# A DFT-plus-MLP kernel: the first-stage output stored as [chunk, residue, feature] instead of [feature, chunk, residue]

## The chip, the cores and the metric

The kernel runs on one core of one Trainium2 chip. The time is the device time of one execution in microseconds (us); lower is better. A profile of one execution stands beside the times.

## The reference, cut to what matters

For each of 8 batches of 3072 rows and 256 features the reference takes a Fourier transform along the rows, then one along the features, and keeps the real part. The 24576 resulting rows go through a small network: the elementwise maximum of three matrix products, then an output product.

```
X = fft(x, axis=1); X = fft(X, axis=2); a = X.real      # x: 8 x 3072 x 256
h = max(a @ w1, a @ w2, a @ w3)                         # 256 -> 768
out = h @ w_out                                         # 768 -> 256
```

## The kernel before, in words

The row transform of length 3072 is split as 24 x 128. The feature axis is split into four chunks `g` of 64 features `dl` each. For every batch the function `fnet` does three steps and then the network runs on its result.

First stage (lines 267 to 272). For each of the 64 features, one matmul with 128 columns of `x0` as its weights and the small block matrix `m24blk` as moving data gives 96 numbers per partition: 4 chunks `g` times 24 residues `r`. The weights are taken from `x0` with a step of 64 elements, 128 bytes. Five features (once four) share a PSUM tile `ps1`, and one ScalarE (ACT) copy moves the 480 numbers to the SBUF tile `ub` as bf16. There are 13 such evictions in a batch, in the order of `DLS`, and the PSUM pool `ps_f` has two buffers, so matmul group n+2 waits for eviction n. In `ub` the 96 numbers of a feature lie together.

Folds (lines 279 to 297). VectorE (DVE) adds and subtracts mirrored features: `fold` combines features `lo..hi` of chunk `g` with features `64-lo..64-hi`, backwards, of chunk `3-g`. The sums go to `zE`, the differences to `zO`. There are three rounds (25 features, two times 10, two times 9), each for two chunks, sums before differences; five small operations (lines 289 to 297) finish feature 0.

Second stage (lines 305 to 335). For each residue `r` the 128 folded features of that residue are the weights of a matmul, `er[:, :, r]` or `orr[:, :, r]`, with cosine or sine tables as moving data (128 columns, 64 for two residues). In the layout of before, neighbouring weights of one residue are 24 elements apart in `zE` (48 bytes) and 26 apart in `zO` (52 bytes). There are 50 such matmuls a batch in six PSUM tiles `ps2` of the same pool `ps_f`, each evicted by ACT to `tE` or `tO` (line 329), and three more with one column (lines 332 to 334). GpSimd then makes reversed copies (lines 339 and 340).

The network (`unit_plus`, `unit_minus`, `unit_out`, `l2_half`, `l2_block`) works in three blocks a batch: TensorE fills `pse`, ACT takes a relu to `stmp` (line 363), DVE takes the maximum into `hp` or `hm` (line 364), and the output product accumulates in `po` (lines 367, 369, 372), is copied by DVE to `ot` (line 392) and stored from the SP queue. A scheduler interleaves output-product matmuls of the batch before with the first and second stage of the next batch. Each engine then works through its own list in that order.

At the start DVE and ACT build the tables. The order in which `zE` and `zO` hold the 128 features must match the order in the tables `md`; that order comes from `dvec` (line 130).

Of the kernel before, what the change touches and what calls it, by code (L numbers as in the profile page):

```python
# [34 lines left out]
def kernel(  # L35
# [16 lines left out]
    nc = tc.nc  # L52
# [44 lines left out]
    def load_x0(b, between):  # L97
        x0 = x0_pool.tile([96, 128 * 64], BF16, name="x0", tag="x0")
        xr = x[b].rearrange("(a bb) (g dl) -> g a bb dl", bb=128, g=4)
        x0v = x0.rearrange("p (bb dl) -> p bb dl", dl=64)  # L100
        for ch in range(4):
            if ch in between:
                between[ch]()
            for g in range(4):
                nc.gpsimd.dma_start(  # L105
                    out=x0v[g * 24:(g + 1) * 24, ch * 32:(ch + 1) * 32, :],
                    in_=xr[g, :, ch * 32:(ch + 1) * 32, :])
        return x0
# [15 lines left out]
    dvec = gen.tile([128, 128], FP32, tag="dvec")  # L124

    def between():

        nc.gpsimd.iota(kidx, [[1, 13], [24, 128]], base=0, channel_multiplier=0,
                       allow_small_or_imprecise_dtypes=True)
        nc.gpsimd.iota(dvec, [[1, 64], [64, 2]], base=0, channel_multiplier=0,  # L130
                       allow_small_or_imprecise_dtypes=True)

    with tc.manual_schedule(engines={mybir.EngineType.Pool}):
# [3 lines left out]
        for jh in range(2):  # L137
            for wsrc, wdst in ((moe_w1, w1_bf), (moe_w2, w2_bf), (moe_w3, w3_bf)):
                nc.gpsimd.dma_start(
                    out=wdst.rearrange("p (fc j) -> p fc j", fc=2)[:, :, jh * 384:(jh + 1) * 384],  # L140
                    in_=wsrc.rearrange("(fc p) j -> p fc j", fc=2)[:, :, jh * 384:(jh + 1) * 384])
        nc.gpsimd.dma_start(out=wout_bf.rearrange("p (jc c) -> p jc c", jc=NJC),
                            in_=moe_w_out.rearrange("(jc p) c -> p jc c", jc=NJC))
# [5 lines left out]
    for thr in (48, 24):  # L149
# [3 lines left out]
                                   in1=pidx[0:96], op0=ALU.mult, op1=ALU.add)  # L153
# [60 lines left out]
    zO_tiles = [consts.tile([128, 128 * 26], BF16, name=f"zO{i}", tag=f"zO{i}")  # L214
                for i in range(1)]
    for zO in zO_tiles:
        nc.vector.memset(zO.rearrange("p (c r) -> p c r", r=26)[:, :, 24:26], 0.0)
        nc.vector.memset(zO[:, 0:26], 0.0)

    def prep_first():  # L220

# [42 lines left out]
    def fnet(b, x0):  # L264
        x0r = x0.rearrange("p (bb dl) -> p bb dl", dl=64)
        ub = u_pool.tile([128, 64 * 96], BF16, name="ub", tag="ub")
        for (d0, d1) in DLS:
            ps1 = ps_f.tile([128, 512], FP32, name="ps1", tag="ps")
            for i in range(d1 - d0):
                nc.tensor.matmul(ps1[:, i * 96:(i + 1) * 96], x0r[:, :, d0 + i], m24blk,  # L270
                                 start=True, stop=True)
            nc.scalar.copy(out=ub[:, d0 * 96:d1 * 96], in_=ps1[:, 0:(d1 - d0) * 96])  # L272

        u = ub.rearrange("p (dl g r) -> p dl g r", g=4, r=24)
        zE = z_pool.tile([128, 128 * 24], BF16, name="zE", tag="zE")
        zO = zO_tiles[b % len(zO_tiles)]
        e = zE.rearrange("p (dl g r) -> p dl g r", g=2, r=24)
        o = zO.rearrange("p (dl g r) -> p dl g r", g=2, r=26)
        def fold(dst, op, lo, hi, g):
            nc.vector.tensor_tensor(out=dst[:, lo:hi, g, 0:24], in0=u[:, lo:hi, g, :],  # L280
                                    in1=u[:, 64 - lo:64 - hi:-1, 3 - g, :], op=op)

        for ranges in (((20, 45),), ((10, 20), (45, 55)), ((1, 10), (55, 64))):
            for (dst, op) in ((e, ALU.add), (o, ALU.subtract)):
                for (lo, hi) in ranges:
                    for g in range(2):
                        fold(dst, op, lo, hi, g)
                if ranges[0][0] == 1:
                    nc.vector.tensor_tensor(out=dst[:, 0, 1, 0:24], in0=u[:, 0, 1, :],
                                            in1=u[:, 0, 3, :], op=op)  # L290
                    if dst is e:
                        nc.vector.tensor_copy(e[:, 0, 0, :], u[:, 0, 0, :])

        nc.vector.tensor_scalar(out=o[:, 0, 0, 1:12], in0=u[:, 0, 2, 13:24], scalar1=-1.0,
                                scalar2=None, op0=ALU.mult)
        nc.vector.tensor_copy(o[:, 0, 0, 13:24], u[:, 0, 2, 1:12])
        nc.vector.tensor_copy(o[:, 0, 0, 24:26], u[:, 0, 2, 0:13:12])

        er = zE.rearrange("p (c r) -> p c r", r=24)
        orr = zO.rearrange("p (c r) -> p c r", r=26)  # L300

        def iO(r):
            return 24 if r == 0 else 25 if r == 12 else 12 + r

        tE = t_pool.tile([128, NHALF], BF16, name="tE", tag="tE")
        tO = t_pool.tile([128, NHALF], BF16, name="tO", tag="tO")
        for (tile_i, dst) in ((0, tE), (1, tO)):
            for g in range(3):
                parts = [(r, r * 128, 128) for r in range(4 * g + 1, min(4 * g + 5, 12))]
                if g == 2:  # L310
                    parts += [(0, 0, 64), (12, 12 * 128, 64)]
                ps2 = ps_f.tile([128, 512], FP32, name="ps2", tag="ps")
                c0 = 0
                for (r, k0, w) in parts:
                    outsl = ps2[:, c0:c0 + w]
                    if tile_i == 0:
                        two = 1 <= r <= 11
                        nc.tensor.matmul(outsl, er[:, :, r], cos_t[:, k0:k0 + w],  # L318
                                         start=True, stop=not two)
                        if two:  # L320
                            nc.tensor.matmul(outsl, er[:, :, 12 + r], sin_t[:, k0:k0 + w],  # L321
                                             start=False, stop=True)
                    else:
                        nc.tensor.matmul(outsl, orr[:, :, r], nsin_t[:, k0:k0 + w],  # L324
                                         start=True, stop=False)
                        nc.tensor.matmul(outsl, orr[:, :, iO(r)], cos_t[:, k0:k0 + w],  # L326
                                         start=False, stop=True)
                    c0 += w
                nc.scalar.copy(out=dst[:, g * 512:(g + 1) * 512], in_=ps2)  # L329

        ps3 = ps_f.tile([128, 512], FP32, name="ps3", tag="ps")
        nc.tensor.matmul(ps3[:, 0:1], er[:, :, 0], cos_t[:, 64:65], start=True, stop=True)
        nc.tensor.matmul(ps3[:, 1:2], orr[:, :, 0], nsin_t[:, 64:65], start=True, stop=False)
        nc.tensor.matmul(ps3[:, 1:2], orr[:, :, 24], cos_t[:, 64:65], start=False, stop=True)
        nc.scalar.copy(out=t_mid[:, :, b], in_=ps3[:, 0:2])

        tEr = t_pool.tile([128, NHALF], BF16, name="tEr", tag="tEr")
        tOr = t_pool.tile([128, NHALF], BF16, name="tOr", tag="tOr")
        nc.gpsimd.tensor_copy(tEr, tE[:, ::-1])  # L339
        nc.gpsimd.tensor_copy(tOr, tO[:, ::-1])  # L340
        return (tE, tO), (tEr, tOr)
# [83 lines left out]

    for b in range(B):
        tt = fnet(b, x0_tiles.pop(b))
        if b == 0:
            prep_first()
# [60 lines left out]
```

## Time and profile before

| | us |
|---|---|
| median of three runs | 500.57 |
| lowest, highest | 499.67, 501.51 |
| span of the profiled execution | 497.1 |
| PE busy, share of the span | 453.5, 91% |
| DVE busy | 320.4, 64% |
| ACT busy | 260.9, 52% |
| POOL busy | 140.6, 28% |

The span runs from the first to the last instruction of the profiled execution. No separate total was recorded for that execution; the median of the runs stands 3.5 us above its span, for what lies around it. In the rows of the profile, PE is a TensorE matmul and PEld a weight load; a group row gives line, engine, operation, output and inputs with their shapes, the count, then the busy time in us and the mean of one in ns, then the idle time of the engine just before and what ended it. In a timeline row the first two numbers are the start and the duration in us; where several instructions are merged (x2), the duration is from the first start to the last end.

### The profile page before, as it was taken

To read this page: it belongs to the slowest core of one execution; us is meant where nothing else is said; L and a number is where in the kernel's file an instruction comes from. 1 tells how busy PE (TensorE), PEld (TensorE's weight loads), DVE (VectorE), ACT (ScalarE), POOL (GpSimd) and SP (SyncE) were. 2 spreads that over 40 slices of the span, in tenths; PEclk is the share of its full clock that TensorE was granted. 3 is DMA by queue.
4 is the path that set the end of the run, shared out by engine and by line. 5 is a ranking of instruction groups with operands and counts; after the bars stand their busy time and mean duration, and the time that the engine had idled before them with its cause. 6 is when DMAs were issued, how large, how long until landed. Compare 5 with 4: busy or idle time off the path is not lost.

```text
span 497.1 us, 9195 instructions
## 1 busy us (share of the span) xinstructions
PE 453.5 (91%) x3408; PEld 315.6 (63%) x3408; DVE 320.4 (64%) x662; ACT 260.9 (52%) x472; POOL 140.6 (28%) x160
## 2 busy tenths in 40 slices
PE   0056999999999999999999999999999999999995
PEld 0055447785568657785669666875669566866664
DVE  8834674657676576657666567657675666667663
ACT  1355652575436653575446644665457644765440
POOL 9979800029000750029000840048000100020000
PEclk9999899999999999999999999999999999999998
DMA  8999992219921692219911793119911022102122
GB/s 48 75 164 99 98 32 86 84 44 108 105 86 66 59 133 99 73 44 109 126 65 65 74 123 102 65 46 120 134 64 65 22 65 84 65 22 65 65 84 86
DMA packets 163436, 40.05 MB, mean 81 GB/s; under 512 B 136512, under 2 KB 163392, under 8 KB 163392
## 3 DMA queue, kind: packets, MB, share of 16 engines
q0 software_dynamic: 135536, 14.30, 70.6%
q1 hardware_dynamic: 27856, 25.18, 16.1%
q8 instruction: 26, 0.43, 0.4%
q14 instruction: 18, 0.15, 0.1%
HBM read 28.31 MB, written 25.17 MB: 108 GB/s over the span
## 4 chain that ended last, share of the span: by engine, by line
PE 78%; DVE 3%; ACT 2%; POOL 2%; DMA 1%; issue 1%; DVEq 0%; ACTq 0%
PE po L372 23%; PE pse L349 12%; PE pse L357 11%; PE pse L350 11%; PE ps L270 8%; PE po L367 4%; PE po L369 4%; POOL x L105 2%; PE ps L318 2%; DMA x<-in_x_dram 1%; PE ps L324 1%; PE ps L326 1%; ACT stmp L363 1%; PE ps L321 1%; DVE zE L280 1%
## 5 line engine op out<-in xcount | busy, mean ns | idle before, releaser
L363 ACT ACTIVATE stmp<-pse 128x512 bf16<-128x512 f32 (+1 forms) x294 | 167.7, 588 | 164.3 <-PE pse L350 128.6
L364 DVE TENSOR_TENSOR hp<-pse,stmp 128x512 bf16<-128x512 f32 x144 | 99.1, 690 | 99.1 <-PE pse L357 39.8
L105 POOL DMA_DIRECT2D x<-in_x_dram x128 | 109.5, 863 | 8.1 <-DMA x<-in_x_dram 3.6
L349 PE MATMUL pse<-tE,gE 128*128 128x512 bf16 x288 | 108.8, 379 | 1.7 <-DVE hm L364 0.7
L350 PE MATMUL pse<-tO,gO 128*128 128x512 bf16 x288 | 109.1, 380 | 0.0
L364 DVE TENSOR_TENSOR hm<-pse,stmp 128x512 bf16<-128x512 f32 x144 | 99.0, 687 | 11.8 <-ACT stmp L363 9.3
L357 PE MATMUL pse<-tO,gD 128*128 128x512 bf16 x288 | 94.8, 380 | 1.1 <-ACT stmp L363 0.6
L339 POOL COPY tEr<-tE 128x1536 bf16<-128x1536 bf16 x8 | 11.8, 1471 | 289.1 <-ACT tE L329 289.1
L372 PE MATMUL po<-wout_bf,hp 128*128 128x256 bf16 x576 | 92.6, 272 | 0.0
L372 PE MATMUL po<-wout_bf,hm 128*128 128x256 bf16 x576 | 89.1, 272 | 0.1
L270 PE MATMUL ps<-m24blk,x 96*128 96x96 bf16 x512 | 57.4, 250 | 28.8 <-DMA w_bf<-in_moe_w_dram 27.5
L270 PEld LDWEIGHTS <-x 96*128 96x128 bf16 x512 | 55.9, 199 | 33.1 <-DMA w_bf<-in_moe_w_dram 27.4
L392 DVE COPY ot<-po 128x512 f32<-128x512 f32 x96 | 65.5, 684 | 14.5 <-PE po L372 13.8
L372 PEld LDWEIGHTS <-hm 128*128 128x128 bf16 x576 | 56.1, 99 | 17.3 <-DVE hm L364 0.4
L372 PEld LDWEIGHTS <-hp 128*128 128x128 bf16 x576 | 56.2, 100 | 14.2
L272 ACT CAST ub<-ps 128x480 bf16<-128x480 f32 (+1 forms) x104 | 55.4, 554 | 15.6 <-PE ps L270 13.3
L357 PEld LDWEIGHTS <-gD 128*128 128x128 bf16 x288 | 28.1, 98 | 29.8 <-issue 1.5
L350 PEld LDWEIGHTS <-gO 128*128 128x128 bf16 x300 | 29.4, 98 | 27.1 <-issue 12.2
L349 PEld LDWEIGHTS <-gE 128*128 128x128 bf16 x300 | 29.5, 99 | 21.1 <-issue 2.6
L280 DVE TENSOR_TENSOR zE<-ub 128x240 bf16<-128x240 bf16 (+2 forms) x80 | 20.2, 311 | 33.9 <-ACT ub L272 33.9
L367 PE MATMUL po<-gw,tE 128*128 128x256 bf16 x96 | 26.2, 272 | 0.0
L369 PE MATMUL po<-gwr,tOr 128*128 128x256 bf16 x96 | 26.2, 272 | 0.0
(99 smaller groups left out, 359.5 us busy)
## 6 DMA issues: line engine op xcount, KB each, us to landing
out_dram<-ot SPq DMA_DIRECT2D x176, 128.0 KB, 1.7
x<-in_x_dram POOLq DMA_DIRECT2D x128, 96.0 KB, 6.7
out_dram<-ot SPq DMA_DIRECT2D x24, 64.0 KB, 6.7
w_bf<-in_moe_w_dram POOLq DMA_DIRECT2D x6, 192.0 KB, 6.2
out_dram<-ot SPq DMA_DIRECT2D x8, 63.0 KB
wout_bf<-in_moe_w_out_dram POOLq DMA_DIRECT2D x1, 384.0 KB, 8.6
out_dram<-ot SPq DMA_DIRECT2D x1, 8.0 KB
```

The source lines that it names most:

```text
L105: nc.gpsimd.dma_start(out=x0v[g * 24:(g + 1) * 24, ch * 32:(ch + 1) * 32, :], in_=xr[g, :, ch * 32:(ch + 1) * 32, :])
L270: nc.tensor.matmul(ps1[:, i * 96:(i + 1) * 96], x0r[:, :, d0 + i], m24blk, start=True, stop=True)
L272: nc.scalar.copy(out=ub[:, d0 * 96:d1 * 96], in_=ps1[:, 0:(d1 - d0) * 96])
L349: nc.tensor.matmul(pse[:, 0:n], gE[i][:, js], te, start=True, stop=False)
L350: nc.tensor.matmul(pse[:, 0:n], gO[i][:, js], to, start=False, stop=True)
L357: nc.tensor.matmul(pse, gD[i][:, js], to, start=False, stop=True, skip_group_check=True)
L363: nc.scalar.activation(out=stmp[:, 0:n], in_=pses[0][:, 0:n], func=AX.Relu)
L364: nc.vector.tensor_tensor(out=dst, in0=src3, in1=stmp[:, 0:n], op=ALU.max)
L367: nc.tensor.matmul(po, te, gw[:, 0:256], start=True, stop=False)
L369: nc.tensor.matmul(po, to, wo, start=False, stop=False)
L372: nc.tensor.matmul(po, hcols(jc), wout_bf[:, jc * 256:(jc + 1) * 256], start=False, stop=(jc == NJC - 1))
L392: nc.vector.tensor_copy(out=ot, in_=po)
```

## The change

`ub` becomes [chunk, residue, feature], so that the 64 features of one chunk and residue lie together. ACT still reads a PSUM tile from end to end but now writes each number 64 elements (128 bytes) from the one before. `zE` and `zO` become [residue, feature]: the 128 weights of one residue lie together. The fold's innermost loop runs over features instead of residues: its rows have 25, 10 or 9 elements instead of 24, and its second input runs backwards with step -1 inside a row. The number of instructions of every kind is unchanged. The memsets of the constant parts of `zO` and the feature order in `dvec` follow the layout.

```diff
-        nc.gpsimd.iota(dvec, [[1, 64], [64, 2]], base=0, channel_multiplier=0,
+        nc.gpsimd.iota(dvec, [[1, 128]], base=0, channel_multiplier=0,
...
-        nc.vector.memset(zO.rearrange("p (c r) -> p c r", r=26)[:, :, 24:26], 0.0)
-        nc.vector.memset(zO[:, 0:26], 0.0)
+        zOr = zO.rearrange("p (r c) -> p r c", c=128)
+        nc.vector.memset(zOr[:, 24:26, :], 0.0)
+        nc.vector.memset(zOr[:, :, 0:1], 0.0)
...
+        ubd = ub.rearrange("p (gr dl) -> p dl gr", dl=64)
...
-            nc.scalar.copy(out=ub[:, d0 * 96:d1 * 96], in_=ps1[:, 0:(d1 - d0) * 96])
-
-        u = ub.rearrange("p (dl g r) -> p dl g r", g=4, r=24)
+            nc.scalar.copy(out=ubd[:, d0:d1, :],
+                           in_=ps1[:, 0:(d1 - d0) * 96].rearrange("p (dl gr) -> p dl gr", gr=96))
+
+        u = ub.rearrange("p (g r dl) -> p dl g r", g=4, r=24)
...
-        e = zE.rearrange("p (dl g r) -> p dl g r", g=2, r=24)
-        o = zO.rearrange("p (dl g r) -> p dl g r", g=2, r=26)
+        e = zE.rearrange("p (r g dl) -> p dl g r", g=2, dl=64)
+        o = zO.rearrange("p (r g dl) -> p dl g r", g=2, dl=64)
         def fold(dst, op, lo, hi, g):
-            nc.vector.tensor_tensor(out=dst[:, lo:hi, g, 0:24], in0=u[:, lo:hi, g, :],
-                                    in1=u[:, 64 - lo:64 - hi:-1, 3 - g, :], op=op)
+            nc.vector.tensor_tensor(
+                out=dst[:, lo:hi, g, 0:24].rearrange("p dl r -> p r dl"),
+                in0=u[:, lo:hi, g, :].rearrange("p dl r -> p r dl"),
+                in1=u[:, 64 - lo:64 - hi:-1, 3 - g, :].rearrange("p dl r -> p r dl"), op=op)
...
-        er = zE.rearrange("p (c r) -> p c r", r=24)
-        orr = zO.rearrange("p (c r) -> p c r", r=26)
+        er = zE.rearrange("p (r c) -> p c r", c=128)
+        orr = zO.rearrange("p (r c) -> p c r", c=128)
```

## The prediction

> **What bounds the kernel now.** I read first the chain that ended last, then who waited for whom, then the groups with their shapes kept apart, and last the timeline of the first and second stage of two batches. The chain:
>
> ```profile
> PE 78%; DVE 3%; ACT 2%; POOL 2%; DMA 1%; issue 1%; DVEq 0%; ACTq 0%
> ```
>
> TensorE is the bound: nearly all of the end is set by its own work, and in the middle of the kernel it hardly idles. So a matmul that starts sooner is worth its whole time, and any new wait of PE costs its whole length. Two waits show where PE meets the changed code:
>
> ```profile
> PE ps L270 <- ACT ub L272: 1.3, 6, 0.3
> PEld L318 <- DVE zE L292: 4.7, 8, 1.8
> ```
>
> Columns are total us, times, longest. The first is PE waiting for an eviction before it can refill `ps_f`; the second is the second stage waiting for the last sums, in every batch. Both are short now and both have no cover left.
>
> The timeline (start, duration) of batch 0, where nothing is interleaved, then of the third batch, then two loads of neighbouring weights from the end:
>
> ```profile
> 28.15 1.02 ACT L272 CAST ub<-ps 128x480 bf16<-128x480 f32 x2 [5.09 <-PE ps L270]
> 28.76 1.06 PE L270 MATMUL ps<-m24blk,x 96*128 96x96 bf16 x10 [0.21 <-ACT ub L272]
> 29.40 1.02 ACT L272 CAST ub<-ps 128x480 bf16<-128x480 f32 x2 [0.22 <-PE ps L270]
> ```
>
> ```profile
> 152.04 1.02 ACT L272 CAST ub<-ps 128x480 bf16<-128x480 f32 x2
> 153.19 0.56 PEld L270 LDWEIGHTS <-x 96*128 96x128 bf16 x5
> 153.62 0.19 PEld L372 LDWEIGHTS <-hp 128*128 128x128 bf16 x2
> 159.65 0.56 ACT L272 CAST ub<-ps 128x480 bf16<-128x480 f32 x1 [0.29 <-PE ps L270]
> 161.27 0.15 PEld L318 LDWEIGHTS <-zE 128*128 128x128 bf16 x1 [0.41 <-DVE zE L292]
> 162.38 0.11 PEld L372 LDWEIGHTS <-hp 128*128 128x128 bf16 x1
> 480.39 0.17 PE L349 MATMUL pse<-t_mid,gE 128*128 128x8 bf16 x1
> 480.42 0.17 PE L350 MATMUL pse<-t_mid,gO 128*128 128x8 bf16 x1
> ```
>
> The loop of the first stage can be read off batch 0. The first eviction of a pair ends at 28.71; PE starts the next ten matmuls 0.05 us later; ACT gets the first of them at 29.40, which is 0.64 us on. A pair of evictions therefore takes 0.56 + 0.05 + 0.64 = 1.25 us, and 13 evictions 6.5 x 1.25 = 8.1 us. The third batch takes the same: 152.04 to 159.65 + 0.56 is 8.2. ACT is busy for 1.02 of each 1.25 us, so it is close to being the bound of this stage.
>
> The groups that I price from:
>
> ```profile
> L272 ACT CAST ub<-ps 128x480 bf16<-128x480 f32 x96 | 52.0, 560 | 15.6 <-PE ps L270 13.3
> L272 ACT CAST ub<-ps 128x384 bf16<-128x384 f32 x8 | 3.9, 481 | 0.0
> L280 DVE TENSOR_TENSOR zE<-ub 128x600 bf16<-128x600 bf16 x16 | 6.8, 468 | 24.5 <-ACT ub L272 24.5
> L280 DVE TENSOR_TENSOR zE<-ub 128x216 bf16<-128x216 bf16 x32 | 6.5, 266 | 6.6 <-ACT ub L272 6.6
> L364 DVE TENSOR_TENSOR hm<-pse,stmp 128x512 bf16<-128x512 f32 x144 | 99.0, 687 | 11.8 <-ACT stmp L363 9.3
> L217 DVE MEMSET zO<- 128x128 uint32 x1 | 0.2, 165 | 0.1
> L218 DVE MEMSET zO<- 128x13 uint32 x1 | 0.1, 69 | 0.0
> L122 DVE MEMSET neg_pi<- 128x1 f32 x1 | 0.1, 59 | 0.8 <-PEq L474 0.8
> ```
>
> **The change part by part.** The built program has the same instructions in the same order on every engine, with the same waits; only addresses and steps move. No DMA and no queue is touched.
>
> *Second stage, removed cost.* Its weight loads of 48- and 52-byte steps stand (162.38 - 161.27) / 16 = 69 ns apart. Neighbouring weights, at 480.39 and 480.42, stand about 32 ns apart with a matmul of 8 columns; a matmul of 256 columns runs every 109 ns (the product matmuls of line 372), so one of 128 should take about 55. Per batch 44 matmuls fall from 69 to 55 ns (0.62 us), six of 64 columns and three of one column from 69 to some 32 (0.33): at most 0.9 us. But each group of eight hands its tile to a 586 ns eviction of line 329 in the same two buffers, and a pair of groups then takes eviction + 0.05 + 8 matmuls + drain, in which only the eight matmuls shrink, 0.11 us a pair, three pairs and the first group: 0.4 us. I take 0.5. Batch 0 gains nothing: its 128-column matmuls stand 107 ns apart whatever the load. 7 x 0.5 = 3.5 us off, between 2.8 and 6.3.
>
> *First stage, added cost.* The two L272 rows give ACT 0.82 ns an element and 165 ns fixed, and two evictions in a row overlap by 0.10 us (2 x 0.56 - 1.02). The new writes step 128 bytes. No ACT row of the trace does that, so let the 0.82 grow by a factor k: an eviction takes E = 165 + 395k ns, and a pair takes E + 0.69 us, or 2 (E - 0.10) once E passes 0.89. There is no slack: the loop is a cycle through the eviction.
>
> The near rows disagree on k. For none: the memset of 128 words at 52-byte steps takes 165 ns, 0.83 ns for each word over the 59 of a single word, and that of 13 adjacent words takes 69, also 0.83. For a high price: TensorE's loads. The `x0` weights have just this 128-byte step in bf16 and stand (153.62 - 153.19) / 5 = 86 ns apart against 32 for neighbours, k = 2.7; the `zE` weights at 48 bytes give 69 / 32 = 2.1. These are reads of another engine, but of the same memory, type and step, and there are hundreds of them where the memsets are one each; I take the middle, 2.4, and keep 1 and 2.7 as ends.
>
> With k = 2.4, E = 1.11 us (0.92 for the short one). ACT becomes the bound: 12 x 1.01 + 0.82 + 0.10 = 13.0 us against 8.1, 4.9 more a batch, 39.5 us over eight. At k = 2 it is 3.0 a batch (24 us), at 2.7 it is 6.0 (48 us). All of it reaches PE: behind the last L270 group PE has only some 1.7 us of product matmuls, which the last two evictions and the folds outlast, and PE's list is fixed, so nothing else moves into the hole.
>
> The Trainium skill, Vector Engine (DVE) Microarchitecture Reference, section 5.2, has measured a VectorE stream whose destination alone steps 24 words: 2.50 to 2.51 ns a column against 1.054 for adjacent ones. It speaks against this change where the memset row speaks for it: by the row the evictions stay at 0.56 us and the sum is about -1.5 us; by that page, carried over to ScalarE as an estimate, it is about +37. No run here shows yet which.
>
> *Folds.* 600 elements take 468 ns and 216 take 266, so 0.53 ns an element; an operation on three bf16 operands with a backward step inside its rows is not in the trace (the reversed write of line 364 costs nothing, 687 ns, but it reads PSUM and runs at a lower rate). If the new rows lose the doubled rate, 216 elements take about 115 ns more. Only the last four sums stand between the last eviction and the second stage, with L289 and L292 behind: 0.46 + some 0.05 us, 4.1 us over eight batches. The earlier folds and the differences have DVE idle time before them (24.5 us ahead of the first). Ends 0 and 4.1; I take 2.
>
> *The rest.* The memsets and `dvec` run once, at the start, under a 27.5 us wait for loads: nothing; without that cover some 0.2 us.
>
> *Sum.* 39.5 + 2 - 3.5 = +38.0: a span of 497.1 + 38.0 = 535.1, and with the 3.5 us by which the median stands above the span, 538.6 us.
>
> **Rivals.** *Strided writes are free* (k near 1): evictions stay at 0.56, and 2 - 3.5 leaves 1.5 us off, 499.1; with the folds at their old rate 497.1, at best some 495. For it: the memset rows. Against it: both weight-load rows. It decides below E = 0.59 us: there the loop's 6.5 x 0.03 x 8 = 1.6 us has eaten the gain. *A small price*, k 1.2 to 1.6 (E 0.64 to 0.80 us): 6.5 x 0.16 = 1.0 us a batch in the middle, +8 - 1.5, about 507. *The clock falls as well*: with PE waiting half of the first stage it may run the second stage as in batch 0, 107 ns a matmul instead of about 60: 44 x 0.05 = 2.2 us a batch, 16 more, about 555; for it speaks that batch 0, with PE 85% covered in the first stage, still shows 107; against it the product matmuls that fill the later batches. That the weights stay as slow as before would only take the 3.5 us away, 542.
>
> **How the numbers follow.** Forecast 0.46 (523 to 547), clock falls 0.14 (539 to 565), small price 0.11, free 0.27, the rest 0.02. Free splits into 0.21 faster and 0.06 same, as 499.1 lies near the 0.5% (2.5 us) that a measurement of this kernel can tell from no change. Slower is the rest, 0.73. As free alone exceeds 0.2, the range reaches from its 495 to 565 (k = 2.7, slow folds and the lower clock: 48 + 4.1 - 3.5 + 16 on 500.6); the forecast's own is 523 to 547.
>
> **What would show it.** The L272 row: 560 ns now, about 1110 if I am right, under 630 if the free rival holds. PE's wait for `ub` at L270: 1.3 us now, some 30 or more. L318 to L326: 69 ns apart now, 55 to 60. L280 with 216 elements: 266, or about 380. I am wrong if the L272 row stays, or if it doubles and the stage from first to last eviction still takes 8 us.

## The result and the profile after

The changed kernel takes 649.55 us (648.72 to 650.48, 4 runs) against 500.87 (499.67 to 501.51, 4 runs): 1.2985 times as long, interval 1.2943 to 1.3027. The sign was right; the size was not, 38 us forecast and 149 measured, far beyond the range. The profiled execution of after took 648.72 us with a span of 646.9, so it is 149.8 us longer in its span than the one of before.

The chain that ended last, the waits of PE and the groups of after:

```profile
PE 54%; ACT 32%; DVE 3%; issue 1%; DVEq 0%; ACTq 0%
```

```profile
PE ps L272 <- ACT ub L274: 108.0, 87, 1.9
PEld L323 <- DVE zE L297: 17.8, 8, 4.6
```

```profile
L274 ACT CAST ub<-ps 128x480 bf16<-128x480 f32 x96 | 212.1, 2625 | 2.0 <-PE ps L272 1.9
L274 ACT CAST ub<-ps 128x384 bf16<-128x384 f32 x8 | 17.7, 2215 | 0.0
L283 DVE TENSOR_TENSOR zE<-ub 128x216 bf16<-128x216 bf16 x32 | 7.3, 323 | 49.9 <-ACT ub L274 49.9
```

The eviction of 480 numbers (line 274 now, 272 before) went from 560 to 2625 ns, not to 1110. ACT's part of the chain went from 2% to 32%, and PE now waits 108 us for `ub` where it waited 1.3. The folds of 216 numbers went from 266 to 323 ns.

The timeline of the third batch, its windows and the second stage behind it (in the window row: length, busy time and count of PE, PEld, DVE, ACT and POOL, then the granted clock, DMA share and GB/s):

```profile
184.73 0.55 PE L272 MATMUL ps<-m24blk,x 96*128 96x96 bf16 x5 [1.45 <-ACT ub L274]
186.90 0.60 PE L272 MATMUL ps<-m24blk,x 96*128 96x96 bf16 x5 [1.51 <-ACT ub L274]
...
206.91 1.48 PE L377 MATMUL po<-wout_bf,hm 128*128 128x256 bf16 x6
...
211.30 0.10 PEld L323 LDWEIGHTS <-zE 128*128 128x128 bf16 x1 [1.89 <-DVE zE L297]
212.16 0.10 PEld L377 LDWEIGHTS <-hp 128*128 128x128 bf16 x1
```

```profile
182.00:210.00 28.00, 14.91 (x102) 10.59 (x100) 5.38 (x15) 28.00 (x14) 0.00 (x0) 0.57 0.06 20
```

ACT is busy for all 28.00 us; PE does five matmuls every 2.17 us (184.73, 186.90) and waits 0.9 to 1.5 us between the groups, although product matmuls fill part of the gap. The granted clock in this window is 0.57, and six product matmuls take 1.48 us (line 377, first start to last end), where six took 0.82 before (line 372, at 150.48). Sixteen second-stage loads take 212.16 - 211.30 = 0.86 us, so they stand 54 ns apart instead of 69.

The difference by stages, from the timelines of both executions: the 13 evictions of a batch take 27.7 us instead of 8.1 (182.38 to 210.08 in the third batch, 152.04 to 160.21 before), 19.6 more. Seven batches show 19.5 to 19.6; the second one, whose first eviction runs 18 us ahead of the others in both kernels, shows 18.1. Over eight batches that is +155.2. From the last eviction to the second stage 1.22 us instead of 1.06, +1.3 over eight batches. The second stage itself (from the first to the last of its 50 matmuls) comes to +1.7. The first eviction starts 4.5 us sooner (23.61 instead of 28.15), the network behind batch 0 is 3.6 us shorter, and the remaining network parts are 0.3 shorter. 155.2 + 1.3 + 1.7 - 4.5 - 3.6 - 0.3 = +149.8.

### The profile page after: what moved, and what is told of

Read it like the earlier page. It is cut to its first block, busy times and chain, and to the rows that moved or that the text cites. A ratio compares the mean times of both kernels' runs of the same rounds, so it can differ in the third digit from the quotient of the medians.

```text
span 646.9 us, 9195 instructions
## 1 busy us (share of the span) xinstructions
PE 491.1 (76%) x3408; PEld 325.3 (50%) x3408; DVE 322.0 (50%) x662; ACT 427.1 (66%) x472; POOL 136.6 (21%) x160
## 4 chain that ended last, share of the span: by engine, by line
PE 54%; ACT 32%; DVE 3%; issue 1%; DVEq 0%; ACTq 0%
ACT ub L274 30%; PE po L377 16%; PE pse L354 10%; PE pse L362 9%; PE pse L355 9%; PE po L372 3%; PE po L374 3%; ACT stmp L368 1%; PE ps L323 1%; PE ps L329 1%; PE ps L326 1%; DVE zE L283 1%; PE ps L331 1%; DVE hm L369 1%; DVE hp L369 1%
## 5 line engine op out<-in xcount | busy, mean ns | idle before, releaser
L274 ACT CAST ub<-ps 128x480 bf16<-128x480 f32 (+1 forms) x104 | 221.7, 2594 | 2.0 <-PE ps L272 1.9
L272 PE MATMUL ps<-m24blk,x 96*128 96x96 bf16 x512 | 61.1, 272 | 131.0 <-ACT ub L274 108.0
L272 PEld LDWEIGHTS <-x 96*128 96x128 bf16 x512 | 60.5, 199 | 154.7 <-issue 127.3
L105 POOL DMA_DIRECT2D x<-in_x_dram x128 | 106.1, 837 | 7.7 <-DMA x<-in_x_dram 4.5
L283 DVE TENSOR_TENSOR zE<-ub 128x240 bf16<-128x240 bf16 (+2 forms) x80 | 22.9, 365 | 169.0 <-ACT ub L274 169.0
L377 PE MATMUL po<-wout_bf,hp 128*128 128x256 bf16 x576 | 103.4, 295 | 0.0
L377 PE MATMUL po<-wout_bf,hm 128*128 128x256 bf16 x576 | 99.1, 294 | 0.1
L377 PEld LDWEIGHTS <-hm 128*128 128x128 bf16 x576 | 59.4, 105 | 19.6 <-DVE hm L369 0.4
L377 PEld LDWEIGHTS <-hp 128*128 128x128 bf16 x576 | 59.3, 106 | 16.1
L323 PE MATMUL ps<-cos_t,zE 128*128 128x128 bf16 (+1 forms) x104 | 18.3, 270 | 14.6 <-DVE zE L297 14.4
```

The source lines that it names most:

```text
L105: nc.gpsimd.dma_start(out=x0v[g * 24:(g + 1) * 24, ch * 32:(ch + 1) * 32, :], in_=xr[g, :, ch * 32:(ch + 1) * 32, :])
L274: nc.scalar.copy(out=ubd[:, d0:d1, :], in_=ps1[:, 0:(d1 - d0) * 96].rearrange("p (dl gr) -> p dl gr", gr=96))
L283: nc.vector.tensor_tensor(out=dst[:, lo:hi, g, 0:24].rearrange("p dl r -> p r dl"), in0=u[:, lo:hi, g, :].rearrange("p dl r -> p r dl"), i ...
L377: nc.tensor.matmul(po, hcols(jc), wout_bf[:, jc * 256:(jc + 1) * 256], start=False, stop=(jc == NJC - 1))
```

## The experiments

The theory after the result: ACT pays per piece of SBUF that a lone 2-byte write enters, far more than TensorE pays for reading at the same step, and everything else follows through the two PSUM buffers. The rivals: the rearranged PSUM read or a power-of-two step is the price; the new layout costs through the folds or the second stage; the loop or the lower clock, not the eviction itself, makes the time. The diffs below are shortened: `...` stands for arguments or code left out, some lines that only repeat or follow are not shown, and L marks a line of the kernel that was run.

**e1_steps: the price of a step, alone.** Behind the end of the kernel of before, single copies of 480 numbers from PSUM to bf16 scratch, each twice, first on ACT, then on DVE.

```diff
+        for copy in (nc.scalar.copy, nc.vector.tensor_copy):
+            copy(out=scr[:, 0:480], in_=psp[:, 0:480])                        # L471
+            for s in (2, 4, 6):
+                copy(out=scr[:, 0:480 * s:s], in_=psp[:, 0:480])              # L474
+            for s in (8, 16, 24, 32, 48, 64, 66, 72, 96, 128, 136):
+                copy(out=scr[...step s...], in_=p5)                           # L477
+            for src in (pru, pgr):       # runs of 5 adjacent, 64 apart
+                copy(out=scr[...], in_=src)                                   # L480
+            copy(out=scr[...adjacent], in_=pgr)      # PSUM read 96 apart     # L482
```

> The kernel before, with copies added behind its end: a PSUM tile of 480 float32 numbers goes to a bf16 scratch tile, first by ScalarE, then by VectorE, each form twice. Forms in order: adjacent; each number 2, 4 and 6 elements from the last; five rows of 96 with steps of 8, 16, 24, 32, 48, 64, 66, 72, 96, 128 and 136 elements; 96 runs of five adjacent numbers at a pitch of 64, once from adjacent PSUM and once from PSUM read at a step of 96; adjacent writes from PSUM read at a step of 96. Only the single copies are of interest, not the total. Theory A (each write that lands far from the last one pays, whatever the exact step): ScalarE rises from 0.56 us when adjacent to about 2.6 at 64 and stays within 15% of that at 66, 72, 96, 128, 136; runs of five take 0.56 to 0.9. Theory B (the step of 128 bytes is special, a power of two that always meets the same place): 64 and 128 take about 2.6 us or more, 66, 72 and 96 at most 1.3. Theory C (lone 2-byte writes pay, at any step): a step of 2 elements already takes about 2.6. VectorE: A gives it a like ratio, 4 to 5 times its adjacent rate at 64; if the price is ScalarE's own, it stays within 1.5 times.

Groups of this run, by line as marked in the diff:

```profile
L471 ACT CAST scr<-psp 128x480 bf16<-128x480 f32 x2 | 1.1, 568 | 0.0
L474 ACT CAST scr<-psp 128x480 bf16<-128x480 f32 x6 | 7.4, 1237 | 0.1
L477 ACT CAST scr<-psp 128x480 bf16<-128x480 f32 x22 | 50.9, 2315 | 0.4
L480 ACT CAST scr<-psp 128x480 bf16<-128x480 f32 x4 | 2.4, 596 | 0.1
L482 ACT CAST scr<-psp 128x480 bf16<-128x480 f32 x2 | 1.2, 578 | 0.0
L477 DVE CAST scr<-psp 128x480 bf16<-128x480 f32 x22 | 50.7, 2305 | 0.6
```

Single ACT copies, from the timeline, in ns (mean of two):

| step in bytes | 2 | 4 | 8 | 12 | 16 | 32 | 48 | 64 | 128 | 132 | 192 | 256 |
|---|---|---|---|---|---|---|---|---|---|---|---|---|
| ns | 568 | 711 | 1238 | 1762 | 2297 | 2161 | 2363 | 2264 | 2295 | 2278 | 2562 | 2296 |

The price rises evenly up to 16 bytes. Beyond, it lies between 2161 and 2562, highest at 192 bytes (on DVE too, 2556), for which the run shows no reason. With the 165 ns fixed part of the prediction, (2297 - 165) / 480 = 4.4 ns for each number that has a 16-byte line to itself; at 8 bytes there are 240 lines, 165 + 240 x 4.4 = 1.22 us, and 1.24 was measured. The step of 128 bytes is no worse than 132, so no power of two is at work, and lone 2-byte writes do not pay in full at every step: 711 at 4 bytes. Runs of five (596) and a stepped PSUM read (578) cost next to nothing beside 568, and DVE pays the same as ACT. The row of after, 2625, is this price plus 0.33 us that the single copy does not show.

**e2_runs_read: the new layout, the write order undone.** ACT reads PSUM with a step of 96 numbers and writes runs of five adjacent ones; everything else is as in after.

```diff
-            nc.scalar.copy(out=ubd[:, d0:d1, :],
-                           in_=ps1[...].rearrange("p (dl gr) -> p dl gr", gr=96))
+            nc.scalar.copy(out=ub.rearrange("p (gr dl) -> p gr dl", dl=64)[:, :, d0:d1],
+                           in_=ps1[...].rearrange("p (dl gr) -> p gr dl", gr=96))
```

> The changed kernel with its eviction turned: ScalarE reads the PSUM tile at a step of 96 numbers and writes 96 runs of five adjacent features, the runs 128 bytes apart. The layouts of ub, zE and zO, the folds and the second stage stay as in the changed kernel. Theory A (a write pays for landing far from the last one): only every fifth write pays, 96 x 4.3 ns is at most 0.4 us more than the fixed part, so the L274 row falls from 2625 ns to 560 to 950, the first stage from 27.7 us to 8.1 to 11, and the time to 497 to 525 us. Theory B (the 128-byte step itself): the step between runs is still 128 bytes, so the same range, its upper half. Theory C (lone 2-byte writes): 0.56 us, 496 to 500 us. If the step of 384 bytes on the PSUM side costs as the writes did, the row stays above 1.5 us and the time above 570.

501.04 us, ratio to before 1.0016 (0.9997 to 1.0036): the order of ACT's writes alone carries the whole loss of some 148 us (ACT's stepped PSUM read, which comes with it, is priced in e1 and e3). Layout, folds, memsets and second stage stay as in after.

```profile
L274 ACT CAST ub<-ps 128x480 bf16<-128x480 f32 x96 | 63.6, 723 | 8.9 <-PE ps L272 7.9
```

```profile
PE ps L272 <- ACT ub L274: 2.5, 9, 0.5
```

PE's wait for `ub` fell to 2.5 us, the clock held, the second stage took 3.59 us. The 723 ns is a mean of two kinds: runs of five that cross a 16-byte boundary took 810 to 901 ns by the medians of their groups, runs that do not 589 to 666, and the short eviction, whose runs of four are aligned to 8 bytes, 479. A crossing costs some (856 - 628) / 96 = 2.4 ns a run, by the middles of the two kinds.

**e3_runs_pe: the step moved to PE.** Each matmul writes its 96 numbers with a step of five PSUM words, ACT then reads end to end.

```diff
-                nc.tensor.matmul(ps1[:, i * 96:(i + 1) * 96], x0r[:, :, d0 + i], m24blk,
+                nc.tensor.matmul(ps1[:, i:(d1 - d0) * 96:d1 - d0], x0r[:, :, d0 + i], m24blk,
```

> The changed kernel with the same runs of five, but TensorE puts them in order: each matmul of the first stage writes its 96 results five apart in PSUM (20 bytes), and ScalarE reads the tile from end to end. Theory A: L274 at 560 to 950 ns as in the kernel that reads PSUM at a step, first stage 8.1 to 11 us, 497 to 525 us; where the two differ, the step on the PSUM read side has a price. If TensorE pays for its stepped PSUM writes, L272 matmuls stand more than the present 86 ns apart; at 110 ns a batch loses 64 x 24 ns = 1.5 us, 12 us in all.

502.89 us, ratio 1.0073 (1.005 to 1.0095). The eviction took 721 ns, as in e2 where ACT read with a step: ACT's stepped PSUM read has no price here. The step did cost PE, 302 ns a matmul against 250 in before (423 against 281 in batch 0, 285 against 246 later). In the pace it shows mainly in batch 0, where the first ten matmuls took 1.82 us instead of 1.09; in a later batch five took 0.61 instead of 0.57.

```profile
L272 PE MATMUL ps<-m24blk,x 96*128 96x96 bf16 x512 | 65.6, 302 | 24.7 <-DMA x<-in_x_dram 23.2
```

**e6_half: does the time follow the evictions?** As e2, but every second of the 13 evictions writes as in after.

```diff
+            if DLS.index((d0, d1)) % 2:
+                nc.scalar.copy(out=ubd[:, d0:d1, :], in_=...)          # L275, as after
+                continue
             nc.scalar.copy(out=ub.rearrange(...)[:, :, d0:d1], in_=...) # L278, as e2
```

> The kernel of e2_runs_read with six of the 13 evictions of each batch (every second one) put back to the changed kernel's writes, one number per 128 bytes; both forms fill the same layout. If ACT's writes bound the stage one after the other, ACT needs 5 x 2.13 + 1.75 + 7 x 0.62 = 16.7 us a batch against 9.2 in e2: 60 us more, about 561 us. If the long evictions hide partly behind the matmuls of the next group (two PSUM buffers), less, down to 540; if each also stalls the short ones behind it, more, up to 580.

569.89 us (one run), within the 540 to 580 expected, 9 above its middle estimate. Six of the 13 evictions are stepped: 501.0 + 148.5 x 6 / 13 = 569.6, as it must be if the loss goes with their number. The two kinds are not quite independent:

```profile
L275 ACT CAST ub<-ps 128x480 bf16<-128x480 f32 x40 | 92.6, 2314 | 4.7 <-PE ps L272 4.2
L278 ACT CAST ub<-ps 128x480 bf16<-128x480 f32 x56 | 57.7, 1030 | 3.5 <-PE ps L272 3.4
```

A short copy behind a long one shows 1030 ns instead of 723, and a long one with short neighbours 2314, the price of e1's single copies: the 0.33 us more in after belong to long ones in a row, where each record begins some 0.5 us before the one ahead has ended.

**e5_reads: why the prediction's near rows misled.** Single copies again behind the end of before: 4-byte writes with steps, pairs of bf16, stepped bf16 reads from SBUF, and three memsets of 128 items.

```diff
+            copy(out=scf[:, 0:1920:4], in_=psp[:, 0:480])     # f32, 16 bytes      L476
+            copy(out=scf[...step 64, 128 bytes], in_=p5)      # f32                L479
+            copy(out=scr[...pairs, 48 bytes apart], in_=p2)   # 240 whole words    L481
+            copy(out=adj, in_=scr[:, 0:480])                  # adjacent read      L483
+            copy(out=a5, in_=scr[...step 16, 52, 128 bytes])  # bf16 reads         L488
+        nc.vector.memset(...)    # 128 adjacent words, L490; 128 words at 52 bytes, L492;
+                                 # 128 single bf16 at 52 bytes, L494
```

> The kernel before, with single operations behind its end, ScalarE first, then VectorE, each twice: 480 float32 numbers from PSUM written as float32 adjacent, then with steps of 16, 64 and 128 bytes; written as bf16 in 240 pairs at a pitch of 48 bytes; then 480 bf16 numbers read from SBUF adjacent and at steps of 8, 16, 52 and 128 bytes and written adjacent; last VectorE memsets of 256 adjacent bf16 zeros, of 128 pairs and of 128 single ones at a pitch of 52 bytes. Only the single operations are of interest. Theory A (a price per 16-byte line that a write enters): float32 at all three steps 2.1 to 2.6 us, pairs about 1.2, 240 lines at 4.4 ns. Theory D (writes of less than a 4-byte word pay, since a word must be completed): float32 steps and pairs stay at 0.56 to 0.75 us. Reads: if they cost what the writes cost, 2.1 to 2.6 us at 16, 52 and 128 bytes; if they go as the weight loads of TensorE, on which the prediction leaned, 1.0 to 1.3; if stepped reads are free, 0.57. Memset: under A the pairs at 52 bytes should take some 0.6 us, yet the row of the profile before says 0.165; a repeat at 0.16 to 0.17 means that memsets escape the price.

```profile
L479 ACT COPY scf<-psp 128x480 f32<-128x480 f32 x4 | 3.9, 976 | 0.1
L481 ACT CAST scr<-psp 128x480 bf16<-128x480 f32 x2 | 1.3, 631 | 0.0
L483 ACT COPY adj<-scr 128x480 bf16<-128x480 bf16 x2 | 1.2, 587 | 0.0
L488 ACT COPY adj<-scr 128x480 bf16<-128x480 bf16 x6 | 6.3, 1043 | 0.1
L490 DVE MEMSET scr<- 128x128 uint32 x2 | 0.3, 165 | 0.3 <-DVE hmid L364 0.3
L492 DVE MEMSET scr<- 128x128 uint32 x2 | 0.3, 165 | 0.1
L494 DVE MEMSET scr<- 128x128 bf16 x2 | 0.3, 165 | 0.0
```

A bf16 read with a step of 16, 52 or 128 bytes costs ACT 1043 ns, k = (1043 - 165) / 395 = 2.2, near the 2.1 and 2.7 of TensorE's weight loads: as a proxy for reads they were about right. A stepped whole 4-byte word costs 976, (976 - 165) / 480 = 1.7 ns, and 1.8 at 16 bytes (line 476, 1028 ns), between what either theory expected. Only the lone 2-byte write costs 4.4. And a memset takes 165 ns whether its 128 items are adjacent, stepped words or stepped halves of words, so the memset row of before said nothing about steps, for or against.

**e4_fours: no crossing at all.** As e2, with 16 groups of four features that begin at multiples of four: 8 adjacent bytes, aligned.

```diff
-    DLS = ((20, 25), (25, 30), (30, 35), (35, 40), (40, 45),
-           (15, 20), (45, 50), (10, 15), (50, 55),
-           (5, 10), (55, 60), (60, 64), (0, 5))
+    DLS = ((20, 24), (24, 28), (28, 32), (32, 36), (36, 40), (40, 44), (44, 48),
+           (16, 20), (48, 52), (12, 16), (52, 56), (8, 12),
+           (56, 60), (4, 8), (60, 64), (0, 4))
```

> The kernel of e2_runs_read with 16 groups of four features instead of 13 of five, each starting at a multiple of four, so that a run is 8 bytes and never straddles a 16-byte boundary. In e2 the runs that straddle one took 0.81 to 0.90 us for 480 numbers and those that do not 0.59, and the one group of four took 0.48 for 384. Theory A (the price is per 16-byte line that a write enters, some 4.4 ns, and is hidden where a line gets four or more numbers): all 16 evictions at 0.48 us, a pair of them 0.48 + 0.05 + 0.55 = 1.08 us, first stage 8.3 to 8.9 us against 9.2 in e2 and 8.1 in the kernel before, second stage 3.6, time 497 to 502 us: within 0.5% of the kernel before. Rival (the price depends on the run's length, or on odd starts): evictions of four at other starts take 0.55 to 0.75, time 502 to 510.

492.71 us (491.07 to 494.11), ratio 0.9849 (0.9817 to 0.9882): faster than both kernels, and than the 497 to 502 expected.

```profile
L274 ACT CAST ub<-ps 128x384 bf16<-128x384 f32 x128 | 58.0, 480 | 12.0 <-PE ps L272 11.2
```

480 ns is the 481 that before takes for 384 numbers written end to end: the new layout can be written at full rate. At 4.4 ns a line its 96 lines would have taken 165 + 96 x 4.4 = 587 ns, so runs of whole words do not pay that price. The first stage takes 8.44 to 8.56 us, the second 3.59.

**e8_pairs: per line, or per lone write?** As e4, but ACT writes each pair of features as one whole word and goes on 128 bytes: 192 steps in an eviction.

```diff
-            out=...rearrange("p (gr dl) -> p gr dl", dl=64)[:, :, d0:d1]
+            out=...rearrange("p (gr h two) -> p h gr two", h=32, two=2)[:, d0 // 2:d1 // 2]
```

> The kernel of e4_fours with each eviction turned once more: ScalarE writes pairs of features (one whole 4-byte word) and hops 128 bytes from pair to pair, 192 words for 384 numbers, instead of runs of four. Theory A (every 16-byte line entered costs 4.4 ns): 192 x 4.4 + 165 = 1.0 us an eviction, ACT alone needs 16 x 0.92 = 14.7 us a batch against 8.5, about 541 us. Theory D (whole 4-byte words cost 1.7 ns a line, as the float32 copies of e5 did, and only a line that gets a part of a word costs 4.4): 192 x 1.7 ns lies under the 0.82 ns an element of the engine itself, so evictions of 0.48 to 0.60 us, 491 to 497 us.

496.1 us, ratio 0.9922 (0.9896 to 0.9948). At 4.4 ns a line the eviction would have taken 165 + 192 x 4.4 = 1.01 us; it took 514 ns:

```profile
L274 ACT CAST ub<-ps 128x384 bf16<-128x384 f32 x128 | 63.0, 514 | 9.2 <-PE ps L272 5.9
```

So it is the half-filled word, together with the step, that makes the high price: two adjacent bf16 that fill a word bring a step of 128 bytes nearly down to adjacent writing.

**e7_iota: the start.** The kernel of before with the feature order of after in `dvec` alone.

```diff
-        nc.gpsimd.iota(dvec, [[1, 64], [64, 2]], base=0, channel_multiplier=0,
+        nc.gpsimd.iota(dvec, [[1, 128]], base=0, channel_multiplier=0,
```

> The kernel before with one line of the change: dvec is filled by the one-row iota of the changed kernel, all layouts as before. It leaves the features in a different order in the tables than in zE and zO, so the result is permuted; the work is the same. In every profile of the old iota it takes 862 ns on GpSimd and the first matmul starts at 27.3 to 27.7 us; in every profile of the new one 262 to 270 ns and 22.5 to 24.4 us. If the iota is the cause, since the remaining loads of x are issued behind it on GpSimd and meet the table work of VectorE at another moment, the first matmul starts at 23 to 24 us here too and the time is 495.5 to 497.5 us. If the other lines of the change are the cause (the memsets of zO), it starts at 27.5 us and the time stays at 499.5 to 501.

495.97 us, ratio 0.993 (0.9905 to 0.9955). The group of the iota and the first matmul, first in before, then in this kernel:

```profile
L130 POOL IOTA dvec<- 128x128 f32 x1 | 0.9, 862 | 0.0
27.46 1.01 PE L270 MATMUL ps<-m24blk,x 96*128 96x96 bf16 x9 [27.46 <-DMA w_bf<-in_moe_w_dram]
```

```profile
L130 POOL IOTA dvec<- 128x128 f32 x1 | 0.3, 262 | 0.0
23.26 1.00 PE L270 MATMUL ps<-m24blk,x 96*128 96x96 bf16 x9 [23.26 <-DMA w_bf<-in_moe_w_dram]
```

The iota is 0.60 us shorter and the first matmul 4.2 us sooner; 1.3 us of that are lost again in the network behind batch 0, and the span is 2.9 us shorter. Of the 16 loads of the first batch POOL issues four ahead of the iota and 12 right behind it. The last is issued at 18.15 instead of 22.06 us; the 12 issues take 12.33 us instead of 15.68. The traces show where the 12 differ: one issue in before, against one of six such in this kernel:

```profile
8.88 6.57 POOL L105 DMA_DIRECT2D x<-in_x_dram  x1
```

```profile
9.60 1.24 POOL L105 DMA_DIRECT2D x<-in_x_dram  x1
```

Most issues take 0.81 us. In before, the one of 6.57 us lasts through DVE's six table operations of lines 176 to 180 (9.23 to 15.05 us); here six issues of 1.24 to 1.35 us lie over the same six operations (8.13 to 15.36 us). So the 0.6 us grow to 4 beside the work on the tables. Why one issue outlasts all six there, and they take turns here, is not settled; nothing was run on it.

**e9_fours_old: is e4's gain the grouping?** The kernel of before with the 16 groups of e4 and nothing else.

> The kernel before with the 16 groups of four of e4_fours and nothing else: old layouts, adjacent writes, old iota. It asks how much of e4's gain of some 7.6 us over the kernel before is the grouping. By stages e4 has 4.0 us from its earlier start and 0.44 us a batch from the second stage, and loses 0.37 a batch in the first stage and 0.47 in front of the second: that sums to about -0.5, so some 7 us are not accounted for by these. If they come from the other order in which the scheduler lists TensorE's work with 16 groups, this kernel shows them: 494 to 498 us. If not, it pays for its longer first stage, 500 to 504 us.

499.91 us, ratio 1.0009 (0.9991 to 1.0028). Evictions of 479 ns and a first stage of 8.44 to 8.56 us gain nothing by themselves. So e4's gain over this one, 7.2 us in the medians and 6.6 in the spans, comes from the rest. By stages of the two profiles the start gives 5.1 (of the kind of e7) and the second stages 7 x 0.44 = 3.1, at 3.59 instead of 4.03 us; 1.3 are lost between the last eviction and the second stage.

## Why the prediction was right and where it was wrong

**The failed step is the size of k.** The formula of the loop held; its one unknown did not. From the two rows of after, (2625 - 2215) / 96 = 4.27 ns a number, k = 5.2, where the prediction took 2.4 and closed its range at 2.7. Put into the prediction's own sum, E - 0.10 = 0.065 + 0.395 x 5.2 = 2.12 us, which makes the 13 evictions of a batch 12 x 2.12 + 2.2 = 27.6 us; 27.7 were measured. That is 19.6 more a batch instead of 4.9, and 155 us in all instead of 39.5: 116 too little, which is the error of 111 and more: the sooner start and the shorter network behind batch 0 gave 8 back, and the second stage took 5 of that again. The upper end came from reads (TensorE's weights at the same step) and was used as a bound for writes; e5 shows that such reads do cost k = 2.2 on ACT too, and e1 that writes of lone bf16 cost twice that. Same memory, type and step were taken to be enough; what mattered was that lone 2-byte numbers were written, for whole words written at the same step cost k = (976 - 165) / 395 = 2.1, no more than the reads. No ACT row of before stepped more than two numbers in its writes, so the range needed an end above the dearest read. That end was also added up wrongly: at k = 2.7 the prediction's formula gives 12 x 1.13 + 0.92 + 0.10 = 14.6 us, 6.5 more a batch and 52 in all, not 6.0 and 48. With 52 the range would have ended at 569, still far short.

**The memset rows** were given weight as the sign of a free write. e5 shows that they hold no news. The free rival (0.27) stood on them alone.

**The stepped 4-byte price** of the Trainium skill, Vector Engine (DVE) Microarchitecture Reference, section 5.2, gave +37 in the prediction, as near as the other sum and as wrong, since that page measures whole 4-byte words. Its 1.71 ns for a destination that hops 4 KiB every element agrees with the 1.7 ns of e5 at 64 and 128 bytes; its 2.50 for steps of 24 words was not seen at 16 or 32 words; no run here has 24.

**The overlap** of two evictions was taken as 0.10 us. The pitch of 2.12 under a record of 2.63 shows 0.5. Both numbers belong together: the excess of the row over e1's copy is given back by the overlap.

**The mechanism was right.** The loop goes through the eviction, ACT becomes its bound, all of it reaches PE: PE's wait for `ub` rose by 106.7 us, that of its weight loads for `zE` by 13.1, and PE's busy time by 37.6 (491.1 against 453.5) with the work unchanged.

**The lower clock** was held to be a rival to the forecast; it came with it, as a part. The granted clock in 40 slices of the span, in tenths, before and after:

```profile
PEclk9999899999999999999999999999999999999998
```

```profile
PEclk9999999579975999569985899759995699858999
```

The slices with 5 to 7 lie mostly in the first stages, where PE waits. Three later batches (2, 3 and 4) had the full clock again in the second stage and took 3.59 us; batches 1, 5, 6 and 7 took 4.78 to 4.96, 1.2 to 1.4 us more each, 5 us in all against the 16 of the rival. Within the first stage the low clock costs nothing, as ACT sets the pace: batch 0, with 1.00 granted there, took 27.70 us just as the third batch did at 0.57.

**The second stage** was right in kind: loads 69 to 54 ns apart, 0.44 us a batch at full clock (4.03 to 3.59) against the 0.5 taken. The kernels e2, e3, e4 and e8 keep it; after loses it again to the clock.

**The folds** were right to be small: 266 to 323 ns, and +0.17 us a batch on the path against +0.25 taken; they do not fall to a lower rate as a whole (600 numbers 468 to 498).

**"`dvec`: nothing" was wrong**: the iota alone brings the first matmul 4.2 us sooner and the time down by 3.2 (495.97 against 499.18, e7). The work was called covered by the wait for loads, but POOL itself issues those loads behind it.

## What to carry to other kernels

Ask of every stepped write whether it fills whole 4-byte words: in these runs lone bf16 numbers cost 4.4 ns each once each has a 16-byte line to itself, whole words 1.7 to 1.9, aligned runs of two words nothing extra (e4). Here the transposing eviction did best when it stepped on its PSUM read side and wrote aligned runs, with the tile's grouping chosen so that no run crosses a line (e4). When the only near row is a read and the change is a write, keep the upper end of the range open by at least a factor of two.

## What the runs showed of the hardware that was not expected

Lone 2-byte writes are priced by the 16-byte line, alike on ACT and DVE (2315 and 2305 ns), and whole words cost less (976 to 1036 ns). The Trainium skill, SBUF — State Buffer, section Specifications (TRN2), says that two or more accesses to a 16-byte line are needed for the full rate. That a new line costs agrees with e1, but for lone 2-byte writes two to a line are not enough: a step of 8 bytes still took 1238 ns against 568, and four to a line 711.

ACT's PSUM read with a step of 384 bytes is free (578 against 568), while PE's PSUM write with a step of 20 bytes is not (302 against 250 ns a matmul, mostly in batch 0).

A memset of 128 items takes 165 ns for adjacent words, for words and for halves of words 52 bytes apart.

An iota of 128 numbers took 862 ns with two dimensions of 64 and 2, and 262 with one; the 0.6 us stood ahead of a queue of load issues, one of which then took 6.57 us beside DVE's table work, and became 4.2 us at the first matmul.
